# Attention with hashed buckets, then eight experts: the first expert's slots cut from 512 to 448, and the second expert's gathers moved

## The chip, the cores and the metric

The kernel runs on one core of a Trainium2 chip. The metric is the device time of one execution in microseconds (us), as the median of the runs. The core has a matrix engine (PE, with its weight load PEld), a vector engine (DVE), a scalar engine (ACT), GpSimd (POOL) and SyncE (SP), which issues most transfers. The engines run beside each other, each in its own order, and wait for one another through semaphores.

## The reference

```
# attention, for each of 4 batches x 8 heads, 768 tokens, 64 wide
mask   = bucket(q @ proj)[:, None] == bucket(k @ proj)[None, :]     # 6 sign bits
scores = where(mask, q @ k.T / 8, -1e9)
attn   = exp(scores - max) / (sum + 1e-9)
x      = (attn @ v), heads side by side                             # 3072 tokens x 512

# mixture of experts: each token goes to the one expert with the largest logit
e_idx  = argmax(x @ w_gate)                                         # 8 experts
for e in range(8):
    t = tokens with e_idx == e
    h = maximum(x[t] @ w1[e], 0)                                    # 512 -> 1024
    out[t] = gate[t] * sigmoid(x[t] @ w_output_gate[:, e]) * (h @ w2[e])
```

All of it is float32. The matrix products are held to that precision by splitting each operand into a high and a low half and doing three products (high by high, high by low, low by high).

## The kernel before, in words

The attention takes the first 450 us or so. As each batch is finished, its tokens are given an expert and a rank within that expert, and a table of slots is added up. The experts are then sorted by their token count: the fullest comes first. Each has a fixed number of slots (`CAPS`, the first number of each entry of `WIDTHS`); the tokens beyond it are done in extra rounds in a loop at the end, which is skipped where there are none.

**The first expert (index 0).** 320 of its slots, the near ones, are filled from the first three batches and begin while attention still runs. The rest is far: a block of 128 slots, `rest`. In the kernel before there is a second far block of 64 slots, `more`, for a first expert with more than 448 tokens. It is gathered and turned every time, but its matrix products stand in three branches (`with overflow()`, lines 1366, 1385 and 1426) that are entered only where the first expert has that many. The near slots' second product (`near_down`, 24 matmuls for each of four column blocks) and the far slots' products (`far_up`, 24 matmuls of 512 columns, `far_down`, 24 more) are written one after the other on PE from line 1312 to 1428. Between them stands what the second expert needs: its rows are gathered (`first`, four chunks), turned by PE transposes (`turn`) and split into halves (`halves`); its w1 pieces are loaded and split (`w1_split`: ACT makes the high half, DVE, or POOL where `"l"` is given, the low half). In the text the second expert is expert 1, the third expert 2, and so on.

**Experts 1 to 7 (lines 1432 to 1502).** Each is 192 matmuls for PE: 96 for the first product, in four steps of 24 (`up`, `fp` 0 to 3), and 96 for the second, in two halves of 48 (`down`, `dp` 0 and 1). How many columns a matmul has is chosen at run time by branches (`narrowed`) among an expert's two or three widths. The results go to PSUM blocks `ps_s`, of which there are two. Before a block is used again DVE must have emptied it and set its unused columns to zero (`clear`, line 373). The first product is emptied by ACT (line 421) and DVE (line 424) into `hh` and `hl`; the second by DVE alone, which turns it into `yt` (line 460).

While an expert is multiplied, the rows of the next one are fetched. `slot_rows` (line 326) makes the slot numbers, `idx`, with four small matmuls and one DVE instruction. A chunk of 128 slots is then four gathers of 32 slots on POOL (`gather_part`, line 338, tile `xq`); `gather_some(m)` issues the next m of those that wait in the list `parts`. Then `turned(a)` turns chunk a: a DVE transpose into `xt` (line 351) and a POOL copy that makes the high half (line 354); the low half is a DVE subtraction (line 355), which stands one step later (`split`). The tables `TURN_UP`, `TURN_DOWN` and `STEPS` say at which step each chunk is turned and how many gathers are issued; expert 1 has tables of its own in the kernel before, `LATE_UP` and `LATE_DOWN`, in which its first chunk is turned alone in step 2, the second in step 3, and the third and fourth in the second product.

Each engine executes in the order in which the code is written; nothing is reordered. So an instruction that waits on DVE holds all later ones on DVE.

Of the kernel before, what the change touches and what calls it, by code (L numbers as in the profile page):

```python
# [12 lines left out]
U32 = mybir.dt.uint32  # L13
# [20 lines left out]
WIDTHS = ((512, 448), (480, 448, 428), (448, 420, 404), (416, 400, 384), (384, 376, 364), (384, 364, 348),  # L34
# [9 lines left out]
UPPER = slice(CH // 2, CH)  # L44
# [3 lines left out]
LATE_UP = {2: (0,), 3: (1,)}  # L48
LATE_DOWN = ((2, 0), (None, None), (3, 1)) + TURN_DOWN[3:]
# [21 lines left out]
def lsh_attention_then_moe(  # L71
# [223 lines left out]
    def gather(idx, n=CH, ntok=NTOK, p0=0):  # L295
# [4 lines left out]
        return xg[p0:n], ident[p0:n, p0:n], n - p0  # L300
# [223 lines left out]
    with ExitStack() as actx:  # L524
# [500 lines left out]
        def lead_slots(a, n):  # L1025
# [5 lines left out]
            nc.vector.tensor_reduce(gd, tm, AX.X, ALU.add)  # L1031
            gid = gp.tile([P, len(near)], U32, name="gid0")
            if a == 0:
                nc.vector.tensor_scalar(gid[:, 0:n], gd, -1.0, 0.0, ALU.add, ALU.max)
                return gid
            nc.vector.tensor_scalar(gid[:, 0:2], gd[:, 1:2].broadcast_to([P, 2]), -1.0, 0.0, ALU.add, ALU.max)
            nc.vector.tensor_scalar(gid[UPPER, 0:1], gd[UPPER, 0:1], -1.0, 0.0, ALU.add, ALU.max)
# [241 lines left out]
    with order_ctx:  # L1279
# [12 lines left out]
        def far_up(pu, c0):  # L1292
            for i in range(2):
                fs = slice(i * DM, (i + 1) * DM)
                product(pu[i], [tuple(x[:, cc, c0:c0 + CH] for x in x0) for cc in range(NCC)],
                        [(wh[:, fs], wl[:, fs]) for wh, wl in early["w1"]])

        def far_relu(ps, pu):
            rows = [mp.tile([CH, DM], F32, name="yo", bufs=4) for i in range(2)]
            for i in range(2):  # L1300
                pace[:] = [nc.scalar.activation(rows[i][ps], pu[i][ps], AF.Relu).ins]
            return [rows[f // NCC][ps, f % NCC * P:(f % NCC + 1) * P] for f in range(NFB)]

        def overflow():
            return tc.If(fits[0] < 1)

        def cleared(pool, name, shape, ps=slice(None)):
            t = pool.tile(shape, F32, name=name)
            nc.vector.memset(t[ps], 0.0)
            return t  # L1310
# [24 lines left out]
        gid = sources(mp, tacc)  # L1335
        ch = chunks(1)
# [15 lines left out]
        spill = [spill[:, i] for i in range(2)]  # L1352
        ids = mp.tile([P, E * NCH], F32R, name="ids")
        nc.vector.tensor_scalar(ids, tacc[:, 0].rearrange("p e a -> p (e a)"), -1.0, 0.0, ALU.add, ALU.max)
        mixed_ids = mp.tile([CH, 2], U32, name="mixed_ids")
        mixed_gates = mp.tile([CH, 1], F32, name="mixed_gates")
        for ps, a in ((slice(0, CH // 2), NCH - 1), (UPPER, NCH - 2)):
            nc.vector.tensor_copy(mixed_ids[ps, 0:1], sid[ps, 0, a:a + 1])
            nc.vector.tensor_copy(mixed_gates[ps], tacc[ps, 1, 0, a:a + 1])
        nc.vector.tensor_scalar(mixed_ids[0:CH // 2, 1:2], sid[0:CH // 2, 0, 0:1], 0.0, SKIP, ALU.mult, ALU.add)  # L1360
        nc.vector.tensor_copy(mixed_ids[UPPER, 1:2], sid[UPPER, 0, NCH - 1:NCH])
        pu = [p.tile([CH, DM], F32, name=n) for p, n in ((ps_a, "ps_a"), (ps_m, "ps_m"))]
# [10 lines left out]
        for i in range(2):  # L1373
            pt = ps_t.tile([P, NCC, CH], F32, name="ps_t")
            for k in range(NCC):
                nc.tensor.transpose(pt[:, k], h_rest[NCC * i + k], ident)
            pace[:] = [halves([h[:, NCC * i:NCC * (i + 1), FAR] for h in hs], pt)]
# [42 lines left out]
        for a in range(len(chunks(2))):  # L1420
            fetch(a, 2)
# [4 lines left out]
        with overflow():  # L1426
            far_down(spill, slice(0, CH), range(NFB))
# [164 lines left out]
```

## Time and profile before

| | us |
|---|---|
| median of 3 runs | 732.61 (732.05 to 733.94) |
| the profiled execution | 734.34 |
| its span, first to last instruction | 732.6 |
| PE busy in the span | 715.5 (98%) |
| DVE busy | 519.7 (71%) |
| ACT busy | 462.9 (63%) |
| POOL busy | 394.4 (54%) |

The profiled execution is 1.7 us longer than its span and 1.7 us longer than the median of the runs. PE is busy in almost the whole span; matmuls are pipelined, so the time of a matmul in its sequence is the distance from its start to the next one's start, and not the duration shown. A window row gives for each engine the busy time in a stretch, and after these the TensorE clock that was granted there: 1.00 is 2.4 GHz, 0.50 is 1.2 GHz. A timeline row that ends in brackets tells how long the engine was idle before it, and what released it.

### The profile page before, as it was taken

Reading aid. Unit: us, or ns where it says so; the run is one execution under the profiler, and the core shown is the slowest. Engines: PE = TensorE matmul, PEld = TensorE weight load, DVE = VectorE, ACT = ScalarE, POOL = GpSimd, SP = SyncE. Lnnn points to the kernel's source line nnn. Section 1 sums busy time; section 2 is a strip of 40 time slices with the busy share of each in tenths; the row PEclk is TensorE's granted clock in tenths of the full one; section 3 lists DMA queues with packets and bytes.
Section 4 is the critical chain, followed back from the end, with each engine's and each line's share of the span. In section 5 each row is a group of like instructions: output and inputs, shape, how many; then the busy total and the mean of one; then the engine's idle time right before and its main releaser. Section 6 shows DMA issues by size and latency. Waiting matters only on the chain. (4 is left out here: it accounts for less than half of the span.)

```text
span 732.6 us, 14169 instructions
## 1 busy us (share of the span) xinstructions
PE 715.5 (98%) x4635; PEld 595.1 (81%) x4635; DVE 519.7 (71%) x1160; ACT 462.9 (63%) x988; POOL 394.4 (54%) x451
## 2 busy tenths in 40 slices
PE   8999999999999999999999999999799999999997
PEld 5777777777786776867868779889699999999996
DVE  7877767878877887877999757654565657566750
ACT  8798887878877888887887761454061617153341
POOL 7656554454754545654477452266547684846212
PEclk9999999999999999999999999999899999999999
DMA  4555654554654565566457143565483967658641
GB/s 154 157 130 127 154 135 95 136 143 92 152 134 96 134 144 110 133 136 142 103 134 177 36 110 77 170 191 178 135 271 115 310 203 248 200 212 269 231 136 42
DMA packets 99814, 110.85 MB, mean 151 GB/s; under 512 B 58905, under 2 KB 71609, under 8 KB 99712
## 3 DMA queue, kind: packets, MB, share of 16 engines
q1 hardware_dynamic: 94288, 96.12, 49.9%
q0 software_dynamic: 5280, 13.38, 5.6%
q8 instruction: 61, 1.00, 0.6%
q14 instruction: 41, 0.34, 0.2%
q10 hardware_dynamic: 144, 0.02, 0.0%
HBM read 65.33 MB, written 19.10 MB: 115 GB/s over the span
## 5 line engine op out<-in xcount | busy, mean ns | idle before, releaser
L755 POOL TENSOR_SCALAR sc<-sc,rsum 128x768 f32<-128x768 f32 x192 | 184.9, 977 | 181.3 <-DVE rsum L753 128.2
L775 ACT COPY pts<-ps_t 128x384 f32<-128x384 f32 x375 | 161.4, 482 | 73.8 <-PE ps_t L771 72.7
L723 DVE TENSOR_SCALAR_CACHE_REDUCE sc<-ps_s 128x768 f32<-128x768 f32 x192 | 181.3, 949 | 36.4 <-PE ps_s L719 32.1
L734 ACT ACTIVATE sc<-sc,mn 128x768 f32<-128x768 f32 (+1 forms) x223 | 187.5, 847 | 0.8 <-DVE sc L723 0.7
L771 PE MATMUL ps_t<-ident,sc 128*128 128x128 f32 x1134 | 156.8, 274 | 0.8 <-ACT pts L775 0.4
L771 PEld LDWEIGHTS ps_t<-ident,sc 128*128 128x128 f32 x1134 | 132.6, 140 | 26.3 <-POOL sc L755 12.2
L793 PE MATMUL ps_a<-pts,vt 128*64 128x384 f32 x768 | 130.9, 490 | 0.0
L719 PE MATMUL ps_s<-xr,xl 128*128 128x384 f32 x384 | 114.3, 379 | 1.2 <-DVE sc L723 0.8
L421 ACT ACTIVATE hh<-ps_s 128x768 fp32r<-128x768 f32 (+5 forms) x36 | 27.4, 761 | 139.1 <-issue 68.7
L338 POOL DMA_INDIRECT xq<-x_dram,idx x75 | 89.3, 1191 | 30.9 <-issue 19.6
L793 PEld LDWEIGHTS ps_a<-pts,vt 128*64 128x64 f32 x768 | 52.3, 137 | 65.1 <-issue 57.2
L719 PE MATMUL ps_s<-yr,yl 76*128 76x384 f32 x384 | 99.0, 339 | 0.2 <-DVE yl L661 0.2
L402 PE MATMUL ps_s<-xh,w1h 128*128 128x320 f32 (+7 forms) x256 | 86.7, 339 | 6.6 <-DVE ps_s L373 5.8
L402 PE MATMUL ps_s<-xlo,w1h 128*128 128x320 f32 (+7 forms) x256 | 85.9, 335 | 0.0
L402 PE MATMUL ps_s<-xh,w1l 128*128 128x320 f32 (+7 forms) x256 | 85.6, 334 | 0.0
L402 PE MATMUL ps_s<-hh,w2h 128*128 128x320 f32 (+6 forms) x224 | 75.5, 337 | 0.1
L402 PE MATMUL ps_s<-hl,w2h 128*128 128x320 f32 (+6 forms) x224 | 74.6, 333 | 0.6 <-DVE hl L424 0.6
L402 PE MATMUL ps_s<-hh,w2l 128*128 128x320 f32 (+6 forms) x224 | 74.5, 332 | 0.0
L719 PEld LDWEIGHTS ps_s<-yr,yl 76*128 76x128 f32 x384 | 69.5, 189 | 0.6 <-POOL xl L626 0.5
L424 DVE SCALAR_TENSOR_TENSOR hl<-ps_s,hh 128x768 fp32r<-128x768 f32 (+5 forms) x36 | 32.1, 891 | 50.7 <-ACT hh L421 37.4
L432 POOL DMA_INDIRECT out_dram<-yo,sid x26 | 27.6, 1063 | 69.0 <-ACT yo L481 56.4
L719 PEld LDWEIGHTS ps_s<-xr,xl 128*128 128x128 f32 x384 | 58.0, 191 | 7.6 <-issue 4.8
(256 smaller groups left out, 1020.9 us busy)
## 6 DMA issues: line engine op xcount, KB each, us to landing
w_raw<-in_w_dram SPq DMA_DIRECT2D x36, 512.0 KB
qk<-in_qkT_dram SPq DMA_DIRECT2D x32, 384.0 KB
xh<-in_w_dram SPq DMA_DIRECT2D x14, 512.0 KB
xlo<-in_w_dram SPq DMA_DIRECT2D x14, 512.0 KB
vt<-in_v_dram SPq DMA_DIRECT2D x16, 384.0 KB
xr<-xl SPq DMA_DIRECT2D x30, 192.0 KB
yr<-xl SPq DMA_DIRECT2D x30, 192.0 KB
xr<-yl SPq DMA_DIRECT2D x30, 192.0 KB
```

The lines of the kernel that those rows point to most:

```text
L338: got = nc.gpsimd.indirect_dma_start(out=xq[:, k * P:(k + 1) * P], out_offset=None, in_=x_dram.rearrange("n (a f) -> (n a) f", a=NB32), in ...
L402: nc.tensor.matmul(ps, l, r, start=first and k == 0, stop=last and k == len(pairs) - 1)
L421: pace[:] = [nc.scalar.activation(hh, ph, AF.Relu).ins]
L424: nc.vector.scalar_tensor_tensor(hl, ph, 0.0, f32(hh), ALU.max, ALU.subtract)
L432: sent = nc.gpsimd.indirect_dma_start(**k).ins
L719: nc.tensor.matmul(ss[:, n, 0:HS], l[0:k, qs], r[0:k, n * HS:(n + 1) * HS], start=first, stop=not first)
L723: nc.vector.tensor_scalar(sc, ss[:, :, 0:HS], MASKED, None, ALU.min, ALU.min, accum_out=mn)
L734: nc.scalar.activation(pr, pr, AF.Exp, bias=mn, scale=-1.0, accum_out=total)
L755: nc.gpsimd.tensor_scalar(live[s0 + k], live[s0 + k], rs[:, k:k + 1], 0.0, ALU.mult, ALU.add)
L771: nc.tensor.transpose(tr[:, c], pr[:, (3 * h + c) * P:(3 * h + c + 1) * P], ident)
L775: (nc.vector.tensor_copy if shared and h else nc.scalar.copy)(pts[:, 3 * h:3 * h + 3, t * P:(t + 1) * P], tr)
L793: nc.tensor.matmul(st["av"][j * D:(j + 1) * D], st["v"][:, j, c], blocks[hb][j][:, c], start=(c == 0), stop=(c == NT - 1))
```

## The change

The first expert's second far block of 64 slots is taken out: its gather, its turn, its products in three branches, the cleared PSUM blocks that stood for them, and its scatter. The first expert now has 448 slots, and whatever goes beyond goes through the rounds at the end. Expert 1's slots go from 480 to 448, with widths 448, 436 and 428 where there were 480, 448 and 428. The slot numbers (`slot_rows`) move from the middle of `far_down` to the end of the first expert's third column block, and six gathers for expert 2, which were two behind the middle of `far_down`, now stand in three pairs between `far_up` and the end of `far_down`. The two low halves of w1 that POOL made there go to DVE. Expert 1 uses the same step tables as the others.

```
-WIDTHS = ((512, 448), (480, 448, 428), (448, 420, 404), ...
+WIDTHS = ((448,), (448, 436, 428), (448, 420, 404), ...
-LATE_UP = {2: (0,), 3: (1,)}
-LATE_DOWN = ((2, 0), (None, None), (3, 1)) + TURN_DOWN[3:]
 ...
         rest = gather(gid0[:, 0:1])
-        more = gather(gid0[:, 1:2], CH, NTOK, CH // 2)
 ...
         gid = sources(mp, tacc)
+        ids = mp.tile([P, E * NCH], F32R, name="ids")
+        nc.vector.tensor_scalar(ids, ...)
-        first = [gather(gid[:, 1, a:a + 1], ch[a]) for a in range(2)]
+        first = [gather(gid[:, 1, a:a + 1], ch[a]) for a in range(len(ch))]
         near_back(py, 0)
         turn(rest, x0, 0)
-        near_down(py, 2, 0, 4)
-        turn(more, x0, CH)
-        near_down(py, 2, 4, NFB)
-        first += [gather(gid[:, 1, a:a + 1], ch[a]) for a in range(2, len(ch))]
+        near_down(py, 2, 0, NFB)
+        idx = slot_rows(ids, pick)
+        for a in range(len(chunks(2))):
+            fetch(a, 2)
 ...
-        spill = cleared(ps_s, "ps_s", [P, 2, 512], UPPER)
-        far_up(pu, 0)
-        h_rest = far_relu(slice(0, CH), pu)
-        read_fit(0)
-        with overflow():
-            far_up(spill, CH // 2)
+        rows = [far_up(ps_a.tile([CH, DM], F32, name="ps_a"), 0)]
+        gather_some(2)
+        rows.append(far_up(ps_m.tile([CH, DM], F32, name="ps_m"), 1))
+        gather_some(2)
         xn = new_x()
         turn(first[0], xn, 0)
         turn(first[1], xn, CH)
         near_down(py, 3, 0, 4)
         w1n = [w1_split(wpool, raw[0])]
 ...
-        h_more = far_relu(UPPER, spill)
-        pt = cleared(ps_a, "ps_a", [P, NFB, CH // 2])
-        w1n.append(w1_split(wpool, raw[1], "l"))
+        far_back(0, rows[0])
+        far_back(1, rows[1])
+        gather_some(2)
+        w1n.append(w1_split(wpool, raw[1]))
 ...
-        with overflow():
-            for f in range(NFB):
-                nc.tensor.transpose(pt[:, f], h_more[f], ident[UPPER, UPPER])
 ...
-        w1n.append(w1_split(wpool, raw[1], "l"))
-        halves([h[:, :, UPPER] for h in hs], pt)
-        spill = cleared(ps_a, "ps_a", [CH, DM])
+        w1n.append(w1_split(wpool, raw[1]))
+        read_fit(1)
         py = ps_m.tile([CH, DM], F32, name="ps_m")
-        far_down(py, FAR, range(0, 4))
-        idx = slot_rows(ids, pick)
-        for a in range(len(chunks(2))):
-            fetch(a, 2)
-        gather_some(2)
-        read_fit(1)
-        far_down(py, FAR, range(4, NFB))
-        send_part(py, mixed_gates, mixed_ids[:, 0:1])
-        with overflow():
-            far_down(spill, slice(0, CH), range(NFB))
-        send_part(spill, tacc[:, 1, 0, NCH - 1:NCH], mixed_ids[:, 1:2])
+        far_down(py, range(NFB))
+        send_part(py, mixed_gates, mixed_ids)
 ...
-                for a in (LATE_UP if r == 1 else TURN_UP).get(fp, ()):
+                for a in TURN_UP.get(fp, ()):
```

On POOL, from the gather of the first expert's far rows (`xg<-x_dram,gid`) to expert 1's third step, the kernel before has this order (`xq` is expert 2's rows, the scatters to `out_dram` send finished rows, `xh<-xt` is line 354):

```order
L298 DMA xg<-x_dram,gid_6385 128x512 x2
L322 CAST pick<-ident 128x512
L298 DMA xg<-x_dram,gid 128x512 x3
L298 DMA xg<-x_dram,gid 96x512
L1366 UNCONDITIONAL_BRANCH
L1385 UNCONDITIONAL_BRANCH
L198 TENSOR_TENSOR w1l<-w_raw,w1h 128x1024
L198 TENSOR_TENSOR w1l<-xlo_6752,w1h 128x1024
L338 DMA xq<-x_dram,idx 128x128 x2
L1426 UNCONDITIONAL_BRANCH
L393 UNCONDITIONAL_BRANCH x2
L432 DMA out_dram<-yo,mixed_ids 3072x512 x2
```

and the changed one this (line numbers are three smaller there):

```order
L295 DMA xg<-x_dram,gid_6385 128x512
L319 CAST pick<-ident 128x512
L295 DMA xg<-x_dram,gid 128x512 x3
L295 DMA xg<-x_dram,gid 64x512
L335 DMA xq<-x_dram,idx 128x128 x6
L390 UNCONDITIONAL_BRANCH x2
L429 DMA out_dram<-yo,mixed_ids 3072x512
L335 DMA xq<-x_dram,idx 128x128 x2
```

Six gathers of expert 2 stand ahead of the first scatter where two stood, and the two w1 subtractions and one scatter are gone from POOL.

On DVE, from the third step of expert 1 to the emptying of the first half of its second product (`yt<-ps_s`), the kernel before has:

```order
L424 SCALAR_TENSOR_TENSOR hl<-ps_s,hh 128x960
L393 UNCONDITIONAL_BRANCH
L373 MEMSET ps_s 128x2x52
L355 TENSOR_TENSOR xlo<-xt,xh 128x4x128
L351 STREAM_TRANSPOSE xt<-xq 128x4x4x32
L355 TENSOR_TENSOR xlo<-xt,xh 128x4x128
L351 STREAM_TRANSPOSE xt<-xq 128x4x4x32
L198 TENSOR_TENSOR w1l<-w_raw,w1h 128x1024
L355 TENSOR_TENSOR xlo<-xt,xh 128x4x128
L351 STREAM_TRANSPOSE xt<-xq 128x2x4x32
L198 TENSOR_TENSOR w1l<-w_raw,w1h 128x1024
L460 STREAM_TRANSPOSE yt<-ps_s 128x15x32
```

and the changed one:

```order
L348 STREAM_TRANSPOSE xt<-xq 128x4x4x32 x2
L421 SCALAR_TENSOR_TENSOR hl<-ps_s,hh 128x896
L370 MEMSET ps_s 128x2x20
L352 TENSOR_TENSOR xlo<-xt,xh 128x4x128 x2
L348 STREAM_TRANSPOSE xt<-xq 128x4x4x32
L352 TENSOR_TENSOR xlo<-xt,xh 128x4x128
L348 STREAM_TRANSPOSE xt<-xq 128x2x4x32
L195 TENSOR_TENSOR w1l<-w_raw,w1h 128x1024
L352 TENSOR_TENSOR xlo<-xt,xh 128x4x64
L195 TENSOR_TENSOR w1l<-w_raw,w1h 128x1024
L457 STREAM_TRANSPOSE yt<-ps_s 128x14x32
```

Two chunks instead of one are turned ahead of the last `hl`, and two instead of three behind it.

## Rows read from the trace of the kernel before

**Rows 1.** Windows: busy us (instructions) of five engines, granted clock, DMA share, GB/s.

```profile
520.00:525.00 5.00, 0.06 (x1) 0.09 (x1) 3.65 (x7) 0.00 (x0) 1.29 (x1) 0.83 0.25 61
525.00:530.00 5.00, 5.00 (x15) 4.75 (x16) 3.33 (x5) 0.00 (x0) 3.92 (x4) 0.50 0.71 235
```

**Rows 2.** PE timeline, expert 1 into 2: start, us, operation [idle, releaser].

```profile
519.56 0.36 PE L402 MATMUL ps_s<-hh,w2l 128*128 128x428 f32 x1
524.94 0.69 PE L402 MATMUL ps_s<-xh,w1h 128*128 128x420 f32 x1 [5.02 <-DVE ps_s L373]
...
530.24 0.35 PE L402 MATMUL ps_s<-xh,w1h 128*128 128x420 f32 x1
530.43 0.35 PE L402 MATMUL ps_s<-xlo,w1h 128*128 128x420 f32 x1
```

**Rows 3.** Chain of waits into that gap: start, us, what.

```profile
482.74 18.73 PE ps_s L402 x96
...
514.76 1.50 POOL xh L354
...
518.14 0.96 POOL xq L338
...
523.33 1.24 DVE yt L460 x2
...
524.66 0.14 DVE ps_s L373
```

**Rows 4.** Timeline of DVE, the last chunk's transpose in expert 1.

```profile
520.96 0.62 DVE L351 STREAM_TRANSPOSE xt<-xq 128x256 f32<-128x256 f32 x1 [3.96 <-DMA xq<-x_dram,idx]
```

**Rows 5.** Timeline of POOL, the first gather of expert 2.

```profile
481.80 0.98 POOL L338 DMA_INDIRECT xq<-x_dram,idx  x1
```

**Rows 6.** Timeline of DVE, end of expert 3: its PSUM block is cleared.

```profile
595.85 0.09 DVE L373 MEMSET ps_s<- 128x40 f32 x1
```

**Rows 7.** Timeline of PE, expert 3 into expert 4.

```profile
599.73 0.33 PE L402 MATMUL ps_s<-xh,w1h 128*128 128x376 f32 x1
```

**Rows 8.** Timeline of PE, expert 2 into expert 3.

```profile
563.70 0.36 PE L402 MATMUL ps_s<-hh,w2l 128*128 128x420 f32 x1
564.46 0.42 PE L402 MATMUL ps_s<-xh,w1h 128*128 128x400 f32 x1 [0.40 <-DVE yt L460]
```

**Rows 9.** Timeline of PE, the first expert's far part up to expert 1.

```profile
460.32 0.31 PE L402 MATMUL ps_s<-hh,w2l 128*128 128x320 f32 x1
460.56 0.69 PE L310 MATMUL ps_t<-ident,xg 64*128 64x64 f32 x4
...
461.44 0.31 PE L402 MATMUL ps_s<-hl,w2h 128*128 128x320 f32 x1
461.58 0.31 PE L402 MATMUL ps_s<-hh,w2l 128*128 128x320 f32 x1
...
468.42 0.40 PE L402 MATMUL ps_m<-w1h,xlo 128*128 128x512 f32 x1
469.11 1.22 PE L310 MATMUL ps_t<-ident,xg 128*128 128x128 f32 x8 [0.30 <-PEq L1366]
...
474.40 0.30 PE L402 MATMUL ps_s<-hh,w2l 128*128 128x320 f32 x1
475.09 1.18 PE L310 MATMUL ps_t<-ident,xg 128*128 128x128 f32 x8 [0.38 <-PEq L1385]
...
481.68 0.39 PE L402 MATMUL ps_m<-w2l,hh 128*128 128x512 f32 x1
481.90 0.40 PE L402 MATMUL ps_m<-w2h,hl 128*128 128x512 f32 x1
482.74 0.45 PE L402 MATMUL ps_s<-xh,w1h 128*128 128x428 f32 x1 [0.44 <-PEq L1426]
```

**Rows 10.** Timeline of DVE, one of the w1 subtractions before expert 1.

```profile
471.93 1.23 DVE L198 TENSOR_TENSOR w1l<-w_raw,w1h 128x1024 fp32r<-128x1024 f32 x1
```

**Rows 11.** Timeline of ACT, the third w1 piece of expert 1.

```profile
476.70 1.06 ACT L197 CAST w1h<-xh 128x1024 fp32r<-128x1024 f32 x1
```

More of the change, by code (lines that the diff above doesn't have):

```diff
@@ L31 @@
 NCH = 4
-WIDTHS = ((512, 448), (480, 448, 428), (448, 420, 404), (416, 400, 384), (384, 376, 364), (384, 364, 348),
+WIDTHS = ((448,), (448, 436, 428), (448, 420, 404), (416, 400, 384), (384, 376, 364), (384, 364, 348),
           (384, 356, 340), (368, 336, 312))
@@ L293, in targets, with gather @@
         return sid
-    def gather(idx, n=CH, ntok=NTOK, p0=0):
+    def gather(idx, n=CH, ntok=NTOK):
         xg = gp.tile([CH, DM], F32, name="xg", bufs=NCH)
@@ L299, in gather @@
                                      in_offset=bass.IndirectOffsetOnAxis(ap=idx[0:n], axis=0))
-        return xg[p0:n], ident[p0:n, p0:n], n - p0
+        return xg[0:n], ident[0:n, 0:n], n
     def new_x0():
@@ L1031, in lead_slots @@
             nc.vector.tensor_reduce(gd, tm, AX.X, ALU.add)
+            if a:
+                nc.vector.tensor_copy(gd[0:CH // 2, 0:1], gd[0:CH // 2, 1:2])
             gid = gp.tile([P, len(near)], U32, name="gid0")
[L1033 to L1037, printed above, removed]
+            nc.vector.tensor_scalar(gid[:, 0:n], gd, -1.0, 0.0, ALU.add, ALU.max)
             return gid
@@ L1290, in near_back @@
                                     py[:, j, 0:NEAR].rearrange("p (t i) -> p t i", i=32))
[L1292 to L1310, printed above, removed]
+        def far_up(pu, i):
+            fs = slice(i * DM, (i + 1) * DM)
+            product(pu, [tuple(x[:, cc, 0:CH] for x in x0) for cc in range(NCC)],
+                    [(wh[:, fs], wl[:, fs]) for wh, wl in early["w1"]])
+            row = mp.tile([CH, DM], F32, name="yo", bufs=4)
+            pace[:] = [nc.scalar.activation(row, pu, AF.Relu).ins]
+            return [row[:, k * P:(k + 1) * P] for k in range(NCC)]
@@ new lines, in far_back, with far_down @@
+        def far_back(i, row):
+            pt = ps_t.tile([P, NCC, CH], F32, name="ps_t")
+            for k in range(NCC):
+                nc.tensor.transpose(pt[:, k], row[k], ident)
+            pace[:] = [halves([h[:, NCC * i:NCC * (i + 1), FAR] for h in hs], pt)]
+        def far_down(py, fs):
+            product(py, [(hs[0][:, f, FAR], hs[1][:, f, FAR]) for f in fs], [w2s[f] for f in fs],
+                    fs[0] == 0, fs[-1] == NFB - 1)
+        xgs = {}
+        parts = []
+        whole = []
@@ L1312, in lsh_attention_then_moe, with fetch, gather_some @@
+        def fetch(a, e):
+            if e < E and a < len(chunks(e)):
+                n = chunks(e)[a]
+                for k in range((n + 31) // 32):
+                    parts.append((e, a, n, k))
+        def gather_some(m):
+            for e, a, n, k in parts[:m]:
+                if k == 0:
+                    xgs[e, a] = mp.tile([P, DM], F32, name="xq", bufs=NCH), n
+                gather_part(xgs[e, a][0], idx[:, k, e, a:a + 1], k)
+            del parts[:m]
         back = mp.tile([P, CAP // 32, NCC, 32], F32, name="yt")
@@ L1350, in lsh_attention_then_moe @@
             load_expert(idi, i)
-        spill = cleared(ps_s, "ps_s", [P, 2, 512], UPPER)
[L1352 to L1355, printed above, removed]
+        mixed_ids = mp.tile([CH, 1], U32, name="mixed_ids")
         mixed_gates = mp.tile([CH, 1], F32, name="mixed_gates")
-        for ps, a in ((slice(0, CH // 2), NCH - 1), (UPPER, NCH - 2)):
-            nc.vector.tensor_copy(mixed_ids[ps, 0:1], sid[ps, 0, a:a + 1])
+        for ps, a in ((slice(0, CH // 2), NCH - 1), (slice(CH // 2, CH), NCH - 2)):
+            nc.vector.tensor_copy(mixed_ids[ps], sid[ps, 0, a:a + 1])
             nc.vector.tensor_copy(mixed_gates[ps], tacc[ps, 1, 0, a:a + 1])
-        nc.vector.tensor_scalar(mixed_ids[0:CH // 2, 1:2], sid[0:CH // 2, 0, 0:1], 0.0, SKIP, ALU.mult, ALU.add)
-        nc.vector.tensor_copy(mixed_ids[UPPER, 1:2], sid[UPPER, 0, NCH - 1:NCH])
-        pu = [p.tile([CH, DM], F32, name=n) for p, n in ((ps_a, "ps_a"), (ps_m, "ps_m"))]
-        far_up(pu, 0)
-        h_rest = far_relu(slice(0, CH), pu)
-        read_fit(0)
-        with overflow():
-            far_up(spill, CH // 2)
+        rows = [far_up(ps_a.tile([CH, DM], F32, name="ps_a"), 0)]
+        gather_some(2)
+        rows.append(far_up(ps_m.tile([CH, DM], F32, name="ps_m"), 1))
+        gather_some(2)
         xn = new_x()
@@ L1372, in lsh_attention_then_moe @@
         w1n = [w1_split(wpool, raw[0])]
[L1373 to L1377, printed above, removed]
-        h_more = far_relu(UPPER, spill)
-        pt = cleared(ps_a, "ps_a", [P, NFB, CH // 2])
-        w1n.append(w1_split(wpool, raw[1], "l"))
+        far_back(0, rows[0])
+        far_back(1, rows[1])
+        gather_some(2)
+        w1n.append(w1_split(wpool, raw[1]))
         raw = [w1_load(1, cc) for cc in range(2, NCC)]
@@ L1391, in lsh_attention_then_moe @@
         clear()
-        w1n.append(w1_split(wpool, raw[1], "l"))
-        halves([h[:, :, UPPER] for h in hs], pt)
-        spill = cleared(ps_a, "ps_a", [CH, DM])
+        w1n.append(w1_split(wpool, raw[1]))
+        read_fit(1)
         py = ps_m.tile([CH, DM], F32, name="ps_m")
-        def far_down(py, cols, fs):
-            product(py, [(hs[0][:, f, cols], hs[1][:, f, cols]) for f in fs], [w2s[f] for f in fs],
-                    fs[0] == 0, fs[-1] == NFB - 1)
-        xgs = {}
-        parts = []
-        whole = []
-        def fetch(a, e):
-            if e < E and a < len(chunks(e)):
-                n = chunks(e)[a]
-                for k in range((n + 31) // 32):
-                    parts.append((e, a, n, k))
-        def gather_some(m):
-            for e, a, n, k in parts[:m]:
-                if k == 0:
-                    xgs[e, a] = mp.tile([P, DM], F32, name="xq", bufs=NCH), n
-                gather_part(xgs[e, a][0], idx[:, k, e, a:a + 1], k)
-            del parts[:m]
-        far_down(py, FAR, range(0, 4))
-        idx = slot_rows(ids, pick)
-        for a in range(len(chunks(2))):
-            fetch(a, 2)
-        gather_some(2)
-        read_fit(1)
-        far_down(py, FAR, range(4, NFB))
-        send_part(py, mixed_gates, mixed_ids[:, 0:1])
-        with overflow():
-            far_down(spill, slice(0, CH), range(NFB))
-        send_part(spill, tacc[:, 1, 0, NCH - 1:NCH], mixed_ids[:, 1:2])
+        far_down(py, range(NFB))
+        send_part(py, mixed_gates, mixed_ids)
         over, nri = rounds()
@@ L1479, in hook @@
                     next_w1(cc)
-            hooks = [lambda i=i, h=h: hook(i, *h) for i, h in enumerate(LATE_DOWN if r == 1 else TURN_DOWN)]
+            hooks = [lambda i=i, h=h: hook(i, *h) for i, h in enumerate(TURN_DOWN)]
             def between():
```

2 lines of the change are left out of this document (1 added, 1 removed).

## The prediction

> **What bounds the kernel now.** I read the windows first, then the timeline of PE, then the chain of waits. PE is busy for 715.5 of 732.6 us, so time can be won only where PE stands still, runs at half its clock or does something that goes away. In the part that the change touches there is one large place of the first two kinds. In the windows of the end of expert 1 [rows 1], PE is busy for 0.06 of 5 us, and in the next 5 us it is busy throughout, but at a granted clock of 0.50. The timeline gives the same from start to start [rows 2]: the last matmul of expert 1 starts at 519.56, the first of expert 2 at 524.94, that is 5.38 us where a step is 0.19 (530.24 to 530.43). From 524.94 to 530.24 there are 15 matmuls, 0.35 us each; at 0.19 they would take 2.87 us.
>
> PE waits there for the memset of a PSUM block (line 373). The chain says why that memset is late [rows 3]: it stands on DVE behind the emptying of the first half of expert 1's second product (line 460), which runs at 523.33. PE had finished that half long before: its 96 matmuls of the first product go from 482.74 to 501.5, the second product takes as long again, so its first half ended at about 510.7. DVE was held by the turning of expert 2's chunks: the POOL copy of the third chunk at 514.76, the last gather on POOL only at 518.14, transpose of the fourth at 520.96 after 3.96 us of idling for the gather's data [rows 3, 4]. The gathers are late because the first of them is issued at 481.80 [rows 5], just before expert 1 starts, after the slot numbers, which stand in the middle of the far part.
>
> **The change, part by part.**
>
> *The gap of expert 1.* Six gathers stand ahead of expert 1 instead of two. Two each follow in its four steps, so all fourteen (4 + 4 + 4 + 2 for 448 slots) are issued by the fourth step, at about 500 instead of 518. Expert 1 then goes by the tables of the others, and a later expert shows what these give: at the end of expert 3 the block is cleared at 595.85 and PE asks for it at 599.73, without any idling in the row [rows 6, 7], so 3.9 us to spare. Expert 1 has two more gathers for the next expert than expert 3 (fourteen against twelve), and a gather takes 0.98 us and 0.3 to the next; that is 2.6 us, within the 3.9. I count the whole gap as gone: 5.38 - 0.19 = 5.19 us. From the other side: if the last gather were still what ends the wait, nothing is gained here (0); a loss would need the gathers to come later than now, and every one of them is ahead in order. What is late next, if the gap goes, is PE itself.
>
> *The clock.* The fall to 0.50 follows these 5 us of standing still and nothing else; the shorter stops of PE (0.40 us ahead of expert 3, for one [rows 8]) leave matmuls at full speed behind them. With the gap the 15 slow steps go: 5.30 - 2.87 = 2.43 us. If a stop of some microseconds remains, this may stay: 0 to 2.43.
>
> *The far part before expert 1, on PE.* This stretch has no long wait; what leaves PE's order shortens it one to one. (1) The turn of `more`: from 460.32 to 461.44 there are 1.12 us for two steps of 0.14, so 0.83 us goes [rows 9]. (2) The three branches round the products of `more`, which are not entered (the sequencer goes on with the next transposes, and no matmul stands between). Start to start, less the normal step (0.22 for 512 columns, as from 481.68 to 481.90; 0.15 for 320): 469.11 - 468.42 - 0.22 = 0.47; 475.09 - 474.40 - 0.15 = 0.54; 482.74 - 481.90 - 0.22 = 0.62 [rows 9]. Together 1.63 us. At the third place the branches that choose expert 1's width stay. In front of expert 4 such branches stand alone and PE does not idle at all [rows 7], so I take the whole 0.62; if they are what costs there, 0.62 stays. (3) Expert 1's last chunk has 64 rows instead of 96, the form that took 0.69 us for four transposes at 460.56, where the eight wider ones at 475.09 took 1.18, so four 0.59: minus 0.1 us. (4) The four small matmuls of the slot numbers and the load of the width register only change place: 0, since both stand between matmuls before and after. The sum of this part is 0.83 + 1.63 - 0.1 = 2.36 us, between 1.7 (0.62 stays) and 2.5.
>
> By the Trainium skill (Runtime: NRT & Kernel Launch, Instruction fetch mechanics) a taken branch whose target lies outside the window already fetched makes the engine wait for the fetch. The trace agrees for the three branches of `more`, and not for the width branches, which jump over whole arms of 24 matmuls without a stop in the rows of expert 4. By the rule alone the width branches ahead of expert 1 would keep costing, and the result would be 722.7; I give that one chance in three, inside the likeliest case.
>
> *The other engines before expert 1.* DVE gets two w1 subtractions from POOL, 1.23 us each [rows 10], so 2.5 us between about 470 and 481. It loses there three memsets, the low halves of `more` and of its product, and three small copies. ACT loses the two copies of `more`. The third and fourth w1 piece must be split before PE's matmuls on them, 1.4 and 2.1 us into expert 1; before, the third was cast at 476.70 [rows 11], 6 us ahead of PE's start. I count 0, with a loss of up to 1.5 us if a w1 piece is late by as much as the subtractions take.
>
> *Expert 2 into 3.* There a stop of 564.46 - 563.70 - 0.19 = 0.57 us waits for DVE's emptying too [rows 8], which is late for the same reason: expert 3's gathers start late because expert 2's ended late. With eight of thirteen issued in expert 1 instead of five it goes: 0.57 us, at worst 0.
>
> *The rest.* Attention is not touched. Expert 1's columns stay at 428 (the width taken before), so its matmuls cost the same; ACT's and DVE's emptying of it is 896 instead of 960 wide, hidden behind 4.7 us of matmuls per step. The scatter that leaves POOL had nobody waiting: 0.
>
> The sum: 5.19 + 2.43 + 2.36 + 0.57 = 10.55 us. The profiled execution lies at 734.34, 1.74 us over its span and 1.73 over the median; I take the gain off the median: 732.61 - 10.55 = **722.1 us**.
>
> **Rivals.**
>
> *A. The gap shrinks but stays.* The third pair of early gathers waits for the ACT copy of the far product, POOL has scatters between, and the last chunk again comes late on DVE, so PE stops for 1 to 3 us at the end of expert 1, perhaps with the slow clock behind it. For it: fourteen gathers are more than any later expert has, and the last two are issued only in step four. Against it: the 3.9 us to spare in expert 3. Price: 2 us of gap and about half of the slow steps come back, some 3.5: 725.6.
>
> *B. The gap stays whole.* Then only the far part is won: 732.6 - 2.4 = 730.2. For it: the waits on POOL and DVE alternate chunk by chunk in the chain. Against: the last gather would be issued some 18 us earlier than now.
>
> *C. Slower: the early gathers and the work given to DVE hold up expert 1's start.* The six gathers move their rows while the third and fourth w1 piece are being loaded, and these pieces are then split on a DVE that is nearly full. It decides only if the third piece comes later than its matmul; it has 6 us to spare now [rows 11], still 3.7 if only PE comes earlier. To end above 732.6 it must eat more than 10.5 us: a stop of 8 us plus the slow clock of 2.4 behind it, so a piece cast at about 490. Six gathers of 32 by 512 elements are less than one w1 piece of 128 by 1024 [rows 10], which speaks against that. At a stop of 9 us: 722.1 + 9 + 2.4 = 733.5.
>
> *D. The change doesn't do what it says here: the first expert overflows.* Were it to hold more than 448 tokens, a round would be run with a whole expert's weights, far more than 10 us. But in the kernel before more than 448 would have entered the branch at line 1366 and put 24 matmuls between 468.42 and 469.11 [rows 9]. There are none, so I give this under 0.01.
>
> **How the numbers follow.** The forecast 0.73, A 0.17, B 0.05, C 0.03, and 0.02 that nothing moves, D with it. The likeliest case's own range is 720.8 to 724.5: below by a small share of other stops that vanish with it, above by the 0.62 of the width branches, a late w1 piece and the 0.57. The range that should hold the time 8 times in 10 adds part of A: 720.8 to 726.5. A measurement of this kernel can tell about 0.3% from no change, 2.2 us, so faster means under 730.4: the forecast, A and most of B give 0.93; within 0.3%: 0.04; slower: 0.03.
>
> **What would show it.** In the changed profile PE goes from expert 1 into expert 2 without an idle of over 1 us, the clock of all windows there is 1.00, and the `xq` gathers start at about 466 rather than 481.80. The memset ahead of expert 2 is done some microseconds before PE asks. The three rows that wait for PEq before expert 1 are gone, and the time from the first matmul of column block three to the first of expert 1 is 2.4 us shorter. A stop of PE in front of a w1 piece, or a DVE transpose that waits for the gathers for several microseconds, would show the prediction wrong.

## The result, and the profile after

The changed kernel takes 724.03 us (median of 4 runs, 723.09 to 724.04), the kernel before beside it 732.4; the ratio is 0.9879 (95% interval 0.9861 to 0.9896). 722.1 was forecast, with a range of 720.8 to 726.5. The profiled execution lies at 724.04 with a span of 722.3, against 734.34 and 732.6 before.

The windows of PE around the passage from expert 1 to expert 2 (busy us and instructions of PE, PEld, DVE, ACT and POOL, granted clock, DMA share, GB/s), where PE stood still and then ran at 0.50 before [rows 1]:

```profile
515.00:520.00 5.00, 5.00 (x28) 4.86 (x27) 1.91 (x4) 0.00 (x0) 3.78 (x5) 1.00 0.86 285
520.00:525.00 5.00, 5.00 (x28) 4.83 (x27) 1.44 (x3) 2.49 (x3) 1.28 (x3) 1.00 0.91 214
```

PE is busy throughout, at the full clock. The timeline of PE gives the same for the passage [rows 2], and ahead of expert 1, where three stops stood before [rows 9], for the last step of the far part:

```profile
480.30 0.39 PE L399 MATMUL ps_m<-w2h,hl 128*128 128x512 f32 x1
480.52 0.35 PE L399 MATMUL ps_s<-xh,w1h 128*128 128x428 f32 x1
...
517.44 0.36 PE L399 MATMUL ps_s<-hh,w2l 128*128 128x428 f32 x1
517.63 0.35 PE L399 MATMUL ps_s<-xh,w1h 128*128 128x420 f32 x1
```

Neither passage has an idle in brackets: 0.22 and 0.19 us from start to start, one step each. The gathers of expert 2 on POOL answer to [rows 5], where the first stood at 481.80; the last at 518.14 [rows 3] is now this one:

```profile
466.70 0.96 POOL L335 DMA_INDIRECT xq<-x_dram,idx  x1 [4.59 <-DVE o_armi L1066]
...
505.61 0.95 POOL L335 DMA_INDIRECT xq<-x_dram,idx  x1 [0.30 <-issue]
```

And DVE, which waited 3.96 us for the last chunk [rows 4] and cleared the block only at 524.66 [rows 3]:

```profile
508.43 0.63 DVE L348 STREAM_TRANSPOSE xt<-xq 128x256 f32<-128x256 f32 x1 [0.49 <-DMA xq<-x_dram,idx]
...
511.95 1.17 DVE L457 STREAM_TRANSPOSE yt<-ps_s 128x448 f32<-128x448 f32 x2
513.21 0.13 DVE L370 MEMSET ps_s<- 128x88 f32 x1
```

The block is clear at 513.21 and PE asks for it at 517.63: 4.4 us to spare.

Taken from start to start of the experts in the two timelines of PE, the 10.3 us of span come from here:

| stretch | before | after | saved |
|---|---|---|---|
| start of the span to expert 1 | 482.74 | 480.52 | 2.22 |
| expert 1 with the passage to 2 | 42.20 | 37.11 | 5.09 |
| expert 2 with the passage to 3 | 39.52 | 37.10 | 2.42 |
| expert 3 | 35.27 | 34.58 | 0.69 |
| experts 4 to 7 | 127.25 | 126.23 | 1.02 |
| last matmul to end of span | 5.62 | 6.76 | -1.14 |

### The profile page after: what moved, and what is told of

It reads as the page before. It is cut to its first block, busy times and chain, and to the rows that moved or that the text cites. A ratio compares the mean times of both kernels' runs of the same rounds, so it can differ in the third digit from the quotient of the medians.

```text
span 722.3 us, 14135 instructions
## 1 busy us (share of the span) xinstructions
PE 711.0 (98%) x4631; PEld 592.5 (82%) x4631; DVE 516.1 (71%) x1155; ACT 460.2 (64%) x983; POOL 383.6 (53%) x446
## 4 chain that ended last, share of the span: by engine, by line
PE 71%; issue 12%; POOL 9%; DVE 3%; DMA 2%; ACT 1%; SPq 1%; POOLq 0%; DVEq 0%; ACTq 0%
PE ps_s L716 17%; PE ps_a L790 17%; PE ps_t L768 17%; PE ps_s L399 15%; POOL xq L335 5%; POOL out_dram L429 2%; PE ps_m L572 2%; PE ps_m L399 1%; DMA yo<-y_dram 1%; PE ps_m L824 1%; POOL xh L351 1%; DVE sc L720 1%; DMA xr<-xl 1%; POOL yr L618 1%; ACT sc L731 0%
## 5 line engine op out<-in xcount | busy, mean ns | idle before, releaser
L418 ACT ACTIVATE hh<-ps_s 128x768 fp32r<-128x768 f32 (+4 forms) x36 | 27.2, 755 | 132.7 <-PE ps_s L399 81.9
L335 POOL DMA_INDIRECT xq<-x_dram,idx x75 | 87.1, 1161 | 44.4 <-issue 18.5
L421 DVE SCALAR_TENSOR_TENSOR hl<-ps_s,hh 128x768 fp32r<-128x768 f32 (+4 forms) x36 | 31.8, 884 | 51.4 <-ACT hh L418 45.3
```

The costliest lines, as they stand in the source:

```text
L335: got = nc.gpsimd.indirect_dma_start(out=xq[:, k * P:(k + 1) * P], out_offset=None, in_=x_dram.rearrange("n (a f) -> (n a) f", a=NB32), in ...
L418: pace[:] = [nc.scalar.activation(hh, ph, AF.Relu).ins]
L421: nc.vector.scalar_tensor_tensor(hl, ph, 0.0, f32(hh), ALU.max, ALU.subtract)
```

## The experiments

The theory is that the time at which expert 2's rows arrive sets the end of expert 1: the gathers on POOL hold DVE's transposes, and DVE's own order puts the memset that PE waits for behind them. The rivals were: the order of turning sets it (experiments e1 and e6), the second far block and its branches set it (e2, e3, e9), it is enough that the slot numbers are early (e5, e10). Two side questions came up on the way: the pace of the matmuls and the length of the end. Edits are against the changed kernel where nothing else is said.

**e1_late_gathers.** The slot numbers and two gathers go back to the middle of `far_down`; no other gather stands ahead of expert 1.

```
-        idx = slot_rows(ids, pick)
...
-        gather_some(2)
...
-        gather_some(2)
...
-        gather_some(2)
...
-        far_down(py, range(NFB))
+        far_down(py, range(0, 4))
+        idx = slot_rows(ids, pick)
...
+        gather_some(2)
+        far_down(py, range(4, NFB))
```

> The changed kernel with the slot numbers and the first two gathers of expert 2 back in the middle of the far part's last product, and no other gather before expert 1; the tables of the other experts and the 448 slots stay. Theory (early gathers close the gap): the last gather comes in expert 1's second product again, DVE waits for it, PE stops for 4 to 6 us ahead of expert 2 and runs at 0.50 behind it; 730.5 to 733. Rival one (the step tables close it): no gap, 724 to 725. Rival two (the work of the second far block held the engines): no gap, 724 to 725.

Measured: 730.32 (728.75 to 731.62), ratio to before 0.9963 (0.9948 to 0.9978). The stop is back, in two pieces. Timeline of PE:

```profile
505.34 0.46 PE L399 MATMUL ps_s<-hl,w2h 128*128 128x428 f32 x1 [2.49 <-DVE hl L421]
...
524.32 0.43 PE L399 MATMUL ps_s<-xh,w1h 128*128 128x420 f32 x1 [2.09 <-DVE ps_s L370]
```

The earlier order of turning brings the first chunk's transposes ahead of DVE's last emptying of the first product (`hl`), so a late gather now stops PE there too. DVE waits 4.95, 6.28 and 3.83 us for the gathers' data. The gathers ahead of expert 1 are what counts; of the change nothing else was undone but the earlier slot numbers that they need.

**e2_before_early.** The kernel before, with its second far block and its three branches, but with early slot numbers, six gathers ahead of expert 1 and the ordinary order of turning: the gather part of the change alone. The edit is against the kernel before.

```
+        idx = slot_rows(ids, pick)
...
+        gather_some(4)
...
+        gather_some(2)
...
-                for a in (LATE_UP if r == 1 else TURN_UP).get(fp, ()):
+                for a in TURN_UP.get(fp, ()):
```

> The kernel before, with the second far block and its three branches kept, but with the slot numbers early, six gathers of expert 2 ahead of expert 1, and the tables of the others. Theory: gap, slow clock and the stop ahead of expert 3 are gone, the 2.3 us of the far part stay: 726 to 727. Rival two: the gap stays, 731 to 733.

Measured: 724.27 (723.95 to 724.6), ratio 0.9882 (0.9865 to 0.9898). The stop is gone with the far block still there: the gathers with their slot numbers and the ordinary order of turning give practically all that the change gives. The two subtractions of w1 and both scatters are still on POOL here, so that their going is not the cause either. Expert 1 starts late, as in the kernel before, behind the third of three stops on the branches:

```profile
482.87 0.43 PE L402 MATMUL ps_s<-xh,w1h 128*128 128x428 f32 x1 [0.55 <-PEq L1427]
```

That is 2.35 us later than in the changed kernel, and yet the span is 722.2. The time is some 2 us below the expectation, so the changed kernel loses something elsewhere; e7 looks for it.

**e3_three_branches.** The changed kernel with three branches that are never entered, where `more` had its products, and a register load and a memset ahead of the first.

```
+        with tc.If(fits[0] > 0):
+            for i in range(2):
...
+        with tc.If(fits[0] > 0):
+            for k in range(NCC):
...
+        with tc.If(fits[0] > 0):
+            far_down(spill, range(NFB))
```

> The changed kernel with three branches that are never entered put back at the three places (after the far rows' first product with the load of a register ahead of it, ahead of the last two turned chunks, at the end of the far part), with matmuls inside as before, and one memset of a PSUM block on DVE. Theory: each costs PE 0.3 to 0.6 us, together 1.6: 725.6, and three idles on PE's sequencer. Rival: a branch that is not entered costs nothing, the stops were waits for semaphores of the removed work: 724.0 to 724.4.

Measured: 725.68 (724.45 to 726.07), 1.65 above the changed kernel. Timeline of PE, the three places:

```profile
469.31 1.21 PE L307 MATMUL ps_t<-ident,xg 128*128 128x128 f32 x8 [0.30 <-PEq L1374]
...
475.23 1.34 PE L307 MATMUL ps_t<-ident,xg 128*128 128x128 f32 x8 [0.30 <-PEq L1393]
...
482.79 0.43 PE L399 MATMUL ps_s<-xh,w1h 128*128 128x428 f32 x1 [0.55 <-PEq L1406]
```

From column block three to expert 1 this trace takes 23.61 us, the changed kernel's 21.81: the branches cost PE about what was read off the kernel before (1.63), the last one too. The changed kernel has only the branches of expert 1's width in that last place, and no idle.

**e4_before_again.** The kernel before, unchanged, for a second trace.

> The kernel before once more, for a second trace: the profiled execution of the first was 1.7 us over the median of the runs. Theory: the difference lies in the gap ahead of expert 2 and the slow stretch behind it, which are shorter in a usual run: span about 730.5, gap 3.5 to 4.5 us. Rival: it is spread over attention, and the gap is 5 us again.

Measured: 732.62 (731.56 to 734.11); the stop of 5.14 us at 525.04 is there again. The stop ahead of expert 3, read as 0.57 in the first trace [rows 8], is not: expert 3 starts at 564.02, one step of 0.19 behind the last matmul of expert 2. The profiled run, 734.11, is again the highest of its ten, so whether a usual run has a shorter gap stays open.

**e5_none_early.** The slot numbers early, but none of the gathers.

```
-        gather_some(2)
...
-        gather_some(2)
...
-        gather_some(2)
```

> The changed kernel, with the slot numbers where they now stand but none of the six gathers ahead of expert 1; they are issued in expert 1's own steps instead. Theory (the gathers' times set the gap): in the changed kernel the block ahead of expert 2 is cleared at 513.21 and asked for at 517.63, so 4.4 us to spare; six gathers of some 1.25 us each, 7.5 us, now stand behind one another on POOL after expert 1 has begun, so PE stops for about 3 us, with up to 2.4 us for matmuls at the lower clock behind it: 727 to 730. Rival (it is enough that the slot numbers are early): no stop, 724 to 724.6.

Measured: 733.84 (731.54 to 735.45), ratio 1.0017 (1.0005 to 1.0029): not faster at all. Both ideas were too good. Timeline of PE and, last, one row of DVE's:

```profile
508.60 0.72 PE L399 MATMUL ps_s<-hl,w2h 128*128 128x428 f32 x1 [5.41 <-DVE hl L421]
...
527.62 0.43 PE L399 MATMUL ps_s<-xh,w1h 128*128 128x420 f32 x1 [2.29 <-DVE ps_s L370]
```

```profile
506.50 1.08 DVE L348 STREAM_TRANSPOSE xt<-xq 128x512 f32<-128x512 f32 x1 [7.29 <-DMA xq<-x_dram,idx]
```

My expectation priced one stop, at the end of expert 1, as 4.4 us to spare against 7.5 us of gathers. It overlooked that with this order of turning DVE meets the missing rows already at 499, ahead of `hl`; the matmuls behind both stops run slowly besides (granted clock 0.52 from 505 to 510, 0.75 from 530 to 535).

**e6_early_late_tables.** All six gathers early, but expert 1 turns chunks in the order of the kernel before.

```
+LATE_UP = {2: (0,), 3: (1,)}
+LATE_DOWN = ((2, 0), (None, None), (3, 1)) + TURN_DOWN[3:]
...
+                for a in (LATE_UP if r == 1 else TURN_UP).get(fp, ()):
...
+            hooks = [lambda i=i, h=h: hook(i, *h) for i, h in enumerate(LATE_DOWN if r == 1 else TURN_DOWN)]
```

> The changed kernel with all six gathers ahead of expert 1, but with the order in which expert 1 turned the chunks of the next expert in the kernel before (the first two in its third and fourth step, the other two in its second product). Theory (the gathers' times set the gap): the data are there, DVE does not wait for them, the turning ends one place later, and PE has no stop of over 1 us: 724 to 725. Rival (the order of turning set the gap, and the early gathers only go with it): a stop of 3 to 5 us with the lower clock behind it, 729 to 732.

Measured: 723.74 (722.95 to 724.56), ratio 0.9886 (0.987 to 0.9903). The rival falls: once the data are there, the old order does as well. It only has less to spare; the memset on DVE, against PE's first matmul of expert 2 at 517.69:

```profile
515.44 0.13 DVE L372 MEMSET ps_s<- 128x88 f32 x1
```

2.3 us instead of 4.4.

**e7_cap480 and e12_cap480_again.** One number: the tiles of experts 1 to 7 keep 480 columns a row as before the change, where the changed kernel lays them out for 448.

```
-CAP = max(CAPS[1:])
+CAP = 480
```

> The changed kernel with the tiles of experts 1 to 7 laid out for 480 slots, as before the change, and not 448; columns, matmuls and order are the same. Theory (the distance of the rows in the tile sets the pace of the matmuls): expert 2 takes 18.25 us a half as in e2_before_early, where it took 18.55 in the changed kernel, expert 3 goes the other way (17.50 against 17.29), experts 4 to 7 within 0.3 of either; in sum 0.3 to 0.4 us less, 723.6. Rival (the pace comes from another part of the change): 18.55 and 17.29 again, 724.0.

> e7_cap480 again, beside e11_mixed_rows. Theory: 722.4 again, expert 2 at 18.24 us a half, and from the last matmul to the end of the span 5.4 us as in the first trace. Rival (the 1.3 us below the changed kernel were chance in the end of the span): 723.3 to 723.7.

Measured: 722.41 (721.78 to 723.08) and 722.93 (722.4 to 723.24), ratios 0.9862 (0.9846 to 0.9879) and 0.9859 (0.9834 to 0.9883). Starts of the two halves of expert 2 and of expert 3 on PE, in the changed kernel and then in e12:

```profile
517.63 0.35 PE L399 MATMUL ps_s<-xh,w1h 128*128 128x420 f32 x1
...
536.18 0.35 PE L399 MATMUL ps_s<-hh,w2h 128*128 128x420 f32 x1
...
554.73 0.34 PE L399 MATMUL ps_s<-xh,w1h 128*128 128x400 f32 x1
...
572.02 0.34 PE L399 MATMUL ps_s<-hh,w2h 128*128 128x400 f32 x1
```

```profile
518.44 0.35 PE L399 MATMUL ps_s<-xh,w1h 128*128 128x420 f32 x1
...
536.68 0.35 PE L399 MATMUL ps_s<-hh,w2h 128*128 128x420 f32 x1
...
554.92 0.35 PE L399 MATMUL ps_s<-xh,w1h 128*128 128x400 f32 x1
...
572.42 0.34 PE L399 MATMUL ps_s<-hh,w2h 128*128 128x400 f32 x1
```

96 matmuls of 420 columns take 18.55 us with rows of 448 and 18.24 with rows of 480; of 400 columns, 17.29 and 17.50. The kernel before had 480, so the change moved this pace without meaning to. Over the experts that is some 0.4 us; the larger part of the gain of e7 is in the end of the span (below).

**e8_after_again.** The changed kernel, unchanged, for a second trace.

> The changed kernel again, for a second trace. Theory: 724.0, PE without a stop from expert 1 into expert 2, and from the last matmul to the end of the span 6.8 us as in the first trace, where other kernels of this study have 5.2 to 6.5. Rival (the length of the end varies from execution to execution): another length between 5.2 and 6.8 with the same program.

Measured: 723.74 (722.82 to 725.23), span 722.4. Again PE passes from 517.44 to 517.63 without a stop. From the last matmul's start to the end of the span it is 7.1 us, after 6.8 the first time; e7 and e12 have 5.4 and 5.5, the kernel before 5.6 twice. So, as far as two traces each tell, the end goes with the program and not with the execution. It lies in POOL's last drain behind the final scatter. Instructions at the program's end on POOL's queue (ns least/median/most, first and last start), the changed kernel and then e7:

```profile
L1552 POOLq DRAIN  x3: 40/107/3291, 718.2 to 722.1; - x3
```

```profile
L1552 POOLq DRAIN  x3: 40/107/1927, 718.4 to 720.9; - x3
```

What makes it 1.9 us in one and 3.3 in the other, with the same instructions, was not found.

**e9_far_part_alone.** The second far block is gone, but the slot numbers, the gathers and the order of turning are where they were: the other half of the change alone. The edit is that of e1 and that of e6 together.

> The changed kernel with the second far block gone, but with the slot numbers, the two gathers behind them and expert 1's order of turning where they were before the change: the far part of the change alone. Theory: expert 1 begins some 2.3 us earlier than before the change and the stop at its end stays whole, 5 us and the lower clock behind it: 730 to 730.6. Rival (the gathers come late because of the second far block, and its going frees them): no stop, 724 to 725.

Measured: 732.99 (731.46 to 734.08), ratio 0.9995 (0.998 to 1.0009). Both ideas fall: the stop stays and is even longer, and by the medians the far part is worth nothing with it. Timeline of PE, then POOL's first and last gather for expert 2, then the windows of PE behind the stop:

```profile
517.54 0.36 PE L401 MATMUL ps_s<-hh,w2l 128*128 128x428 f32 x1
524.42 0.69 PE L401 MATMUL ps_s<-xh,w1h 128*128 128x420 f32 x1 [6.52 <-DVE ps_s L372]
```

```profile
479.78 0.96 POOL L337 DMA_INDIRECT xq<-x_dram,idx  x1 [17.59 <-DVE over L1082]
...
517.82 0.96 POOL L337 DMA_INDIRECT xq<-x_dram,idx  x1 [0.30 <-issue]
```

```profile
525.00:530.00 5.00, 5.00 (x16) 4.72 (x15) 2.75 (x5) 0.00 (x0) 4.09 (x4) 0.50 0.69 211
530.00:535.00 5.00, 5.00 (x27) 4.84 (x26) 1.88 (x3) 2.81 (x3) 2.38 (x4) 0.96 0.87 264
```

PE comes to the end of expert 1 2.0 us earlier than before [rows 2], and stands there 1.5 us longer. The first gather is 2.0 us earlier as well, the last only 0.3: between them the third chunk's transpose waits 5.31 us for its data, and the fourth chunk's gathers stand on POOL behind the copy of the third. The half us that is left goes into expert 2, whose first half takes 21.32 us where it took 20.71 in the kernel before; 0.31 of this is the pace of its matmuls in rows of 448 (e7).

e1 differs from e9 in the order of turning alone. PE begins expert 2 at the same time in both, 524.32 and 524.42, but where e9 stops once for 6.52 us, e1 stops for 2.49 and for 2.09 us. Behind that second stop its granted clock is 1.00, and the first half of expert 2 takes 18.69 us and not 21.32. So with late gathers the order of turning is not without effect. By the medians it is 2.7 us, which is not firm: e10, whose trace is nearly that of e1, has a median close to that of e9.

**e10_two_early.** Two gathers ahead of expert 1 instead of six.

```
-        gather_some(2)
...
-        gather_some(2)
```

> The changed kernel with two gathers ahead of expert 1 and not six. With none there, e5_none_early stopped for 5.41 and 2.29 us; with six there is no stop. Theory (each early pair takes 2.5 us off the lateness of the later chunks): the first stop falls to about 2.9 us and the second to under 1, with some of the lower clock behind the first: 727.5 to 729.5. Rival (only the first pair matters, as the chunk turned first needs it): no stop of over 1 us, 724 to 725.

Measured: 732.54 (729.4 to 733.4), ratio 0.9989 (0.9973 to 1.0005). Timeline of PE, in a run of 731.37:

```profile
505.34 0.47 PE L399 MATMUL ps_s<-hl,w2h 128*128 128x428 f32 x1 [2.53 <-DVE hl L421]
...
524.45 0.43 PE L399 MATMUL ps_s<-xh,w1h 128*128 128x420 f32 x1 [2.21 <-DVE ps_s L370]
```

The first stop is near what the theory has, the second is not shorter, and the median is 3 us above the top of what I gave. The rival falls all the same: one pair does not do.

The trace is nearly that of e1, whose two gathers stand 13 us later, at 479.62 instead of 466.60, but ahead of expert 1 too. From expert 1's first step on the gathers come at the same times in both (486.50 and 486.54), two for each step. So in these traces what counts is how many stand ahead of expert 1, and not how early those few are: none gives stops of 5.41 and 2.29 us, two some 2.5 and 2.1 to 2.2, six none. Numbers between two and six were not tried. The medians of e1 and e10, 730.32 and 732.54, differ all the same. Four of e10's ten runs show a mean granted clock of 0.993, the profiled one 0.997, so its trace may not show its usual run.

**e11_mixed_rows.** e7 with rows 448 apart, in the same tiles, for experts 3 and 7.

```
+        return [t.rearrange("p k c -> p (k c)")[:, 0:k * 448].rearrange("p (k c) -> p k c", c=448) for t in tiles]
```

> e7_cap480 with the rows of the same tiles laid 448 apart for experts 3 and 7 alone, and 480 for the others. Theory (the distance of the rows sets the pace): a half of expert 3 takes 17.29 us and not 17.50, expert 7 31.29 and not 31.46, the others as in e7_cap480; 0.6 us less than e7_cap480, 721.8. Rival (the place of the tile in the memory sets it): 17.50 and 31.46 again, 722.4.

Measured: 722.92 (721.67 to 723.19), ratio 0.9854 (0.9828 to 0.988). A half of expert 3 on PE takes 17.29 us again:

```profile
554.51 0.35 PE L406 MATMUL ps_s<-xh,w1h 128*128 128x400 f32 x1
...
571.80 0.34 PE L406 MATMUL ps_s<-hh,w2h 128*128 128x400 f32 x1
...
589.09 0.33 PE L406 MATMUL ps_s<-xh,w1h 128*128 128x376 f32 x1
```

Expert 7 takes 31.28. So the distance of the rows, or where they start by it, sets the pace; the tile's place does not. The time is no better than e12's beside it, 722.93: the last matmul starts 1.3 us earlier, but the end of the span is 7.1 us long again instead of 5.5.

The best versions are thus e7 and e11, some 1 us below the changed kernel and 10 below the one before; that 1 us is less than 0.3%, though both medians of e7's program lie below both of the changed kernel's.

## Why the prediction came out right, step by step

**The gap, 5.19 us: right.** The span shows 5.09 for expert 1 with the passage; the missing 0.1 is the pace of the matmuls. Its cause is shown by e1, e5 and e10 (fewer gathers ahead of expert 1 bring stops back), e2 (the gathers with the ordinary order take it away without the rest of the change) and e6 (the old order of turning does not bring it back). The reckoning of the time to spare was off, to the safe side: 3.9 read from expert 3, less 2.6 for two more gathers, leaves 1.3, and 4.4 came. The last gather of expert 2 is not issued by expert 1's fourth step at about 500, as the prediction has it, but at 505.61, when the second product has run since 499.08. Rival A, for which such a late last gather spoke, did not come all the same.

**The clock, 2.43: right. The stop of expert 2, 0.57: there in one execution.** Together 3.00; expert 2 shows 2.42. The difference of 0.58 is the slower pace of 420 columns in rows of 448, which was on no list of mine: expert 2 takes 37.10 us where e12 has 36.48. The 0.57 belongs to the execution that it was read from: in the second trace of the kernel before (e4) this stop is not there, so it could not be counted on for the median.

**The far part, 2.36: right in its place, wrong as a term that can be added to any other.** From the first matmul of column block three to expert 1 it is 2.31 us shorter. The three branches cost about what was read: in e3's trace they make this stretch 1.80 us longer, and its median is 1.65 higher. The 0.62 went whole. The prediction took the rule of the Trainium skill (Runtime: NRT & Kernel Launch, Instruction fetch mechanics) to mean that the width branches would go on costing there. That did not come: they stand between 480.30 and 480.52 without an idle. Nor is it shown, as the prediction says, that the three stops were waits for a fetch. In the trace of the kernel before no DMA packet at all moves from 468.4 to 469.2 us, around the first of them, and around the other two (474.3 to 475.1 and 481.9 to 482.8) none of a queue that carries instructions. What PE waits for at these branches stays open.

The sum added the 2.36 us to the rest as if they could always be had. While the gap is there they are worth 0.0 by the medians (e9): of the 2.1 us by which expert 1 begins earlier, the stop takes back 1.5, and the 0.5 that is left at the start of expert 2 goes in the slower pace and a longer end (6.09 us against 5.62). Rival B, "the gap stays whole", priced at 730.2 by taking them off, would really have been 733. With the gap gone they do count, but the changed kernel hides it. It is only 0.2 us faster than e2 by the medians: expert 1 starts 2.35 us earlier, and 2.45 are given back behind it, 1.52 in the end of the span, about 0.4 by the pace, the rest in small stops of experts 5 and 6 that change places from kernel to kernel. The fairer comparison is e2 against e7 and e12, which all have rows of 480 and ends of 5.2 to 5.5 us. There the far part is worth 1.9 and 1.3 us by the medians; e2's fastest run, 723.95, is slower than the slowest of theirs, 723.24. The stretch from column block three to expert 1 is 2.30 and 1.88 us shorter.

**Rival C, the early gathers hold up expert 1: did not come.** PE goes into expert 1 without an idle, and no matmul of its first product waits for a w1 piece.

**The last 1.9 us.** From profiled execution to profiled execution the gain is 10.30 us, against a sum of 10.55. That these are so near is partly luck: the terms of the sum show 9.82 (5.09, 2.42 and 2.31), and what the sum does not have nearly cancels, 1.71 won in experts 3 to 7 against 1.14 lost in the end and 0.09 ahead of column block three. I took the gain off the median, 1.73 lower than the execution that the sum was read from, and there only 8.4 came. The profiled runs of the kernel before lie at the top of its spread, 734.34 and 734.11, that of the changed kernel at its median. What the highest runs of the kernel before have more than the middle ones was not seen, as no trace of a middle one exists. Of the 48 other runs of that kernel on record beside the experiments, the twelve with a mean granted clock of 0.997 or more took 730.95 to 732.93 us, the others 731.43 to 735.22, so a part of the spread goes with the clock. Kernels which stop for gathers may differ more from run to run: 731.15 to 735.22 for the one before (19 runs beside e9 to e12), 729.4 to 733.4 for e10 (ten runs), against 722.4 to 723.24 for e12 (four runs); but the changed kernel without such a stop went from 722.82 to 725.23 in the four runs of e8. A stop that waits for DMA may simply be shorter in a middle run; that was not shown.

## What to carry to other kernels

Time saved on the engine that is the bound, ahead of a place where it waits for another chain, may be worth little or nothing until that chain is faster (e9): price each part of a change as if it came alone, and the parts together, before adding them up. Where a chain of transfers and turning has to keep step with the matmuls, put more of it ahead of them; an earlier order without earlier data split the stop in two (e1 against e9) and let PE go on no sooner, and only the slow clock behind it was less. And a sum read from one execution is safe only against executions of the same standing; where a kernel's runs spread, expect part of the gain to be the spread.

## What the runs showed that was not expected

- The pace of a matmul goes with the distance of the rows of its moving tile, or with where they start by it: 0.193 us for 420 columns with rows of 448, 0.190 with 480; for 400 columns 0.180 and 0.182; for 376, 0.173 and 0.172.
- The end of the span, behind the last matmul, is 5.2 to 7.1 us in these kernels, the same within 0.4 for one program (6.8 and 7.1; 5.4 and 5.5; 5.6 and 5.6), and no difference in what is done there was found. It is as large as many an effect that a change is made for.
- Behind the longer stops PE ran at a lower granted clock. The windows of 5 us in which these stops end or that follow them show 0.68 (e1, after 2.49 us of standing still), 0.66 (e10, 2.53 us), 0.52 (e5, 5.41 us) and 0.50 (the kernel before, 5.02 us, and e9, 6.52 us), where the two levels are 0.50 and 1.00. Behind stops under 1 us it stayed at 1.00. In between both occur: 2.29 us in e5 were followed by 0.75, 2.21 us in e10 and 2.09 us in e1 by 1.00.
